# K^T V in two row tiles, a finer-grained first group and dummy matmuls, in linear attention followed by an ELU MLP

## The chip, the cores and the metric

The kernel runs on one core of a Trainium2 chip. The metric is the device time of one execution in microseconds (us). The span of a profile is about 2 us shorter than the time measured for the same run, so spans are compared with spans and times with times. Engines: PE is TensorE (matmuls), PEld its weight loads, DVE is VectorE, ACT is ScalarE, POOL is GpSimd, SP issues DMAs. PSUM is the memory that the matmuls write to, in banks. The chain of waits is a view of the profile: the work that ended last, followed back from each step to what released it. The timeline merges neighbouring instructions of one kind into a line; the trace keeps the start of each.

## The reference

```python
# q, k, v: (8 batches, 8 heads, 576 rows, 64); w_in: (512, 2048); w_out: (2048, 512)
kv  = einsum('bhsd,bhse->bhde', k, v)               # K^T V, 64x64 per head
out = einsum('bhsd,bhde->bhse', q, kv)
out = out / sqrt(mean(out*out, -1) + 1e-6) * g_norm # RMS norm per head
x   = out.transpose(0, 2, 1, 3).reshape(4608, 512)
h   = x @ w_in
g   = where(h > 0, h, exp(min(h, 0)) - 1)           # ELU
y   = g @ w_out
```

The kernel computes ELU as max(min(exp(h), 1) - 1, h). Matmul operands are bfloat16, sums float32.

## The kernel before

Work goes in nine groups of 512 rows: groups 0 to 7 are the first 512 rows of each batch, group 8 collects the last 64 rows of all eight. For each group the attention part makes x, transposed; then eight "h tiles" (two blocks of 128 of the 2,048 inner columns each) are computed, passed through ELU into gT, and multiplied by W_out ("o matmuls").

K and V of a batch are 576 = 4 x 128 + 64 rows: four full column blocks and a tail of 64 rows, loaded apart and multiplied last. The attention parts share one PSUM tile of two banks (`at`, one buffer), so they follow each other.

```python
def kv():                                  # K^T V of one group
    kv_ps = at_tile(FP32, 0)[:, 0:512].rearrange("p (r e) -> p r e", r=NPAIR)
    for p in range(NPAIR):                 # 4 pairs of heads
        for c in range(J + 1):             # 4 blocks of 128 rows, then the tail
            rows = P if c < J else TAIL    # 128, or 64
            nc.tensor.matmul(kv_ps[:, p, :],
                lhsT=k_sb[0:rows, c, 2*p:2*p+2, :], rhs=v_sb[0:rows, c, 2*p:2*p+2, :],
                start=(c == 0), stop=(c == J))
    ...                                    # diagonal blocks copied to bd_kv

def se(h):                                 # two row blocks of 128: q (K^T V), norm
    se_ps = at_tile(FP32, 0)...            # matmuls
    nc.scalar.activation(sq, se_ps, AF.Square)
    nc.vector.reduce_sum(out=ss, in_=sq...)
    ...                                    # ACT: Ln, Exp -> 1/rms
    nc.vector.tensor_tensor(out=xs..., in0=se_ps..., in1=ss.to_broadcast(...), op=ALU.mult)

def mm1(T, i):                             # h tile i of group T; ps_m1 has 2 buffers
    h_ps = ps_m1.tile([P, 2, G], FP32, name="h_ps", tag="mm1")
    ...                                    # 8 matmuls 128x128 by 128x512
    nc.scalar.activation(e, h_ps, AF.Exp)
    def rest():
        nc.vector.tensor_scalar(out=e, in0=e, ..., op0=ALU.min, op1=ALU.subtract)
        nc.vector.tensor_tensor(out=gT..., in0=e, in1=h_ps, op=ALU.max)

# schedule
at = attention(0)
for n in (1, 0, 2, 4, 6): at[n]()          # q, kv, se0, se1, x of group 0, one after the other
for i in range(8): mm1(0, i)()             # group 0's h loop: nothing else to run
...                                        # six halves of group 0's o with group 1's attention
for T in range(1, NT):                     # later: h of T, o of T-1, attention of T+1
    for i in range(8):
        rest = mm1(T, i); mm2(T - 1, i); rest()
        if i in at: at[i]()                # {0: kv, 1: q, 2: se0, 4: se1, 6: x}
```

Of the kernel before, what the change touches and what calls it, by code (L numbers as in the profile page):

```python
# [16 lines left out]
def kernel(  # L17
# [11 lines left out]

    nc = tc.nc  # L30
# [8 lines left out]
    TAIL = S - G  # L39
# [29 lines left out]
    nc.vector.memset(bd_kv, 0.0)  # L69
# [5 lines left out]
    def stage_tile():  # L75
        return stage.tile([P, 2048], FP32, name="st", tag="st")

    raw = {}

    def fetch_main(name, src, b):  # L80
        st = stage_tile()
        nc.sync.dma_start(
            out=st.rearrange("p (h x) -> p h x", h=H),
            in_=src[b, :, 0:G, :].rearrange("h (p j) d -> p h (j d)", j=J),
        )
        raw[name, b] = st

    def fetch_tail(name, src, b):
        st = stage.tile([TAIL, H, D], FP32, name="stt", tag="stt", bufs=4)
        nc.sync.dma_start(out=st, in_=src[b, :, G:S, :].rearrange("h p d -> p h d"))  # L90
        raw[name + "t", b] = st

    def fetch(b):
        fetch_main("q", q, b)
        fetch_main("k", k, b)
        fetch_tail("k", k, b)
        fetch_main("v", v, b)
        fetch_tail("v", v, b)

    def fetch_q_tails():  # L100
        st = stage_tile()
        sv = st.rearrange("p (i h d) -> p i h d", i=J, h=H)
        for b in range(B):
            nc.sync.dma_start(
                out=sv[(b % 2) * 64 : (b % 2) * 64 + 64, b // 2, :, :],
                in_=q[b, :, G:S, :].rearrange("h p d -> p h d"),
            )
        raw["q", B] = st

    def fetch_w_in(s):  # L110
        st = stage_tile()
        nc.sync.dma_start(
            out=st.rearrange("p (c f) -> p c f", c=KC),
            in_=moe_w_in.rearrange("(c p) f -> p c f", p=P)[:, :, s * 512 : s * 512 + 512],
        )
        raw["wi", s] = st

    def fetch_w_out(s):
        st = stage_tile()
        nc.sync.dma_start(  # L120
            out=st.rearrange("p (c f) -> p c f", c=KC),
            in_=moe_w_out.rearrange("(c p) f -> p c f", p=P)[:, 4 * s : 4 * s + 4, :],
        )
        raw["wo", s] = st

    bf = {}
# [7 lines left out]
    def cast(name, b, engs):  # L134

        t = qkvp.tile([P, J + 1, H, D], BF16, name=f"{name}_bf", tag=name)
        bf[name, b] = t
        st = raw.pop((name, b))
        if b < B:
            sv = st.rearrange("p (h j d) -> p j h d", h=H, j=J)  # L140
        else:
            sv = st.rearrange("p (j h d) -> p j h d", h=H, j=J)
        for j in range(J):
            copy_on(engs[j % len(engs)], t[:, j, :, :], sv[:, j, :, :])
        if name != "q":
            stt = raw.pop((name + "t", b))
            copy_on(engs[-1], t[0:TAIL, J, :, :], stt)

# [12 lines left out]

    def attention(T):
        st = {}

        def at_tile(dtype, n):
            full = ps_at.tile([P, 1024], FP32, name="at", tag="at")
            return full if dtype == FP32 else full.bitcast(BF16)

        def kv():
            if T == B:  # L170
                return
            k_sb, v_sb = bf.pop(("k", T)), bf.pop(("v", T))
            kv_ps = at_tile(FP32, 0)[:, 0:512].rearrange("p (r e) -> p r e", r=NPAIR)
            for p in range(NPAIR):
                for c in range(J + 1):
                    rows = P if c < J else TAIL
                    nc.tensor.matmul(  # L177
                        kv_ps[:, p, :],
                        lhsT=k_sb[0:rows, c, 2 * p : 2 * p + 2, :],
                        rhs=v_sb[0:rows, c, 2 * p : 2 * p + 2, :],  # L180
                        start=(c == 0),
                        stop=(c == J),
                    )
            nc.scalar.copy(bd_kv[0:64, T, :, 0:64], kv_ps[0:64, :, 0:64])
            nc.scalar.copy(bd_kv[64:128, T, :, 64:128], kv_ps[64:128, :, 64:128])

        def q_t():
            q_sb = bf.pop(("q", T))
            qt_ps = at_tile(BF16, 0).rearrange("p (r t) -> p r t", r=NPAIR)
            for p in range(NPAIR):  # L190
                for j in range(J):
                    nc.tensor.transpose(  # L192
                        qt_ps[:, p, j * P : j * P + P],
                        q_sb[:, j, 2 * p : 2 * p + 2, :],
                        ident,
                    )
# [5 lines left out]
        def se(h):  # L202
            def run():
                qT = st["qT"]
                se_ps = at_tile(FP32, 0).rearrange("p (c f) -> p c f", c=2)
                for c in range(2):
                    j = 2 * h + c
                    for p in range(NPAIR):
                        if T < B:
                            nc.tensor.matmul(  # L210
                                se_ps[:, c, p * P : p * P + P],
                                lhsT=qT[:, p, j * P : j * P + P],
                                rhs=bd_kv[:, T, p, :],
                                start=True,
                                stop=True,
                            )
                        else:
                            for l in range(2):
                                nc.tensor.matmul(
                                    se_ps[l * 64 : l * 64 + 64, c, p * P : p * P + P],  # L220
                                    lhsT=qT[:, p, j * P + l * 64 : j * P + l * 64 + 64],
                                    rhs=bd_kv[:, 2 * j + l, p, :],
                                    start=True,
                                    stop=True,
                                )
                sq = attp.tile([P, 2, DM], BF16, name="sq", tag="sq")
                nc.scalar.activation(sq, se_ps, AF.Square)  # L227
                ss = attp.tile([P, 2 * H], FP32, name="ss", tag="ss")
                nc.vector.reduce_sum(  # L229
                    out=ss, in_=sq.rearrange("p c (h e) -> p (c h) e", h=H), axis=AX.X  # L230
                )
                nc.scalar.activation(ss, ss, AF.Ln, bias=eps_col, scale=1.0 / D)  # L232
                nc.scalar.activation(ss, ss, AF.Exp, scale=-0.5)  # L233
                if h == 0:
                    st["xs"] = attp.tile([P, J, DM], BF16, name="xs", tag="xs")
                nc.vector.tensor_tensor(  # L236
                    out=st["xs"][:, 2 * h : 2 * h + 2, :].rearrange(
                        "p c (h e) -> p (c h) e", h=H
                    ),
                    in0=se_ps.rearrange("p c (h e) -> p (c h) e", h=H),  # L240
                    in1=ss.to_broadcast([P, 2 * H, D]),
                    op=ALU.mult,
                )
# [3 lines left out]
        def x_t():  # L247
            xs = st["xs"]
            xt_ps = at_tile(BF16, 0).rearrange("p (r t) -> p r t", r=NPAIR)
# [14 lines left out]
        return {0: kv, 1: q_t, 2: se(0), 4: se(1), 6: x_t}  # L264
# [4 lines left out]
    def mm1(T, i):  # L269
# [4 lines left out]
        for a in range(2):  # L274
            f = 2 * i + a
            for c in range(KC):
                nc.tensor.matmul(  # L277
                    h_ps[:, a, :],
                    lhsT=w_in_sb[:, c, f * P : f * P + P],
                    rhs=x[:, c, :],  # L280
                    start=(c == 0),
                    stop=(c == KC - 1),
                )
        e = mlpt.tile([P, 2, G], BF16, name="elu_e", tag="elu_e")
        nc.scalar.activation(e, h_ps, AF.Exp)  # L285

        def rest():
# [4 lines left out]
                out=gT[T][:, 2 * i : 2 * i + 2, :], in0=e, in1=h_ps, op=ALU.max  # L292
# [6 lines left out]
    def mm2(T, i):  # L299

        j, half = i // 2, i % 2
        if half == 0:
            o_ps[T] = ps_m2.tile([P, DM], FP32, name="o_ps", tag="mm2")
        for f in range(8 * half, 8 * half + 8):
            nc.tensor.matmul(  # L305
                o_ps[T],
# [5 lines left out]
        if half == 1:  # L312
            if j % 2 == 0:
                o_sb[T] = outp.tile([P, 2, DM], FP32, name="o_sb", tag="o")
            nc.scalar.copy(o_sb[T][:, j % 2, :], o_ps[T])  # L315
            if j % 2 == 1:
                store(T, j // 2)

# [18 lines left out]
    fetch(0)  # L337
    for s in range(4):
        fetch_w_in(s)
    cast("q", 0, [Q])  # L340
    cast("k", 0, [V])
    cast("v", 0, [V, A])
    for s in range(4):
        cast_w_in(s, Q)
    for s in range(4):
        fetch_w_out(s)
    fetch(1)
    at = attention(0)
    for n in (1, 0, 2, 4, 6):
        at[n]()  # L350
# [3 lines left out]
    def cast_all(b):  # L354
        cast("q", b, [Q])
        if b < B:
            cast("k", b, [Q])
            cast("v", b, [Q])

    cast_all(1)  # L360
    for i in range(8):
        mm1(0, i)()
    fetch(2)
    at = attention(1)
    for i, n in ((0, None), (1, 1), (2, 0), (3, 2)):
        mm2(0, i)
        if n is not None:
# [57 lines left out]
```

## Time and profile before

Median of three runs: 350.9 us (350.68 to 351.55). The profiled run took 352.89 us; its span is 351.1 us.

| stage | from, us | what sets the time |
|---|---|---|
| no h matmul yet | 0 to 36.8 | loads, then group 0's attention, one operation after the other |
| groups 0 and 1, not yet dense | 36.8 to 111.25 | waits between PE, ACT and DVE; slow TensorE clock in places |
| from group 2's h on | 111.25 to the end | PE without a gap almost from the start |

These are lines of the page: the busy share of PE, and the TensorE clock that the throttle granted, in tenths, in 40 equal slices (8.8 us each).

```profile
PE   0242778939968999999999999999999999999993
PEclk9999999996989999999999999999999999999998
```

PE is full from the fourteenth slice on (114 us). The clock row shows slow stretches in slices 10 (from 79 us) and 12 (from 97 us). It shows full speed at the start, where the matmuls' own durations say otherwise. Lines of the timeline, PE: start in us, duration, engine, line, operation, operands, count, and in brackets how long the engine had been idle and what ended that.

```profile
36.80 5.99 PE L277 MATMUL h_ps<-xT,w_in_sb 128*128 128x512 bf16 x16 [0.84 <-DVE xT L259]
43.60 1.89 PE L277 MATMUL h_ps<-xT,w_in_sb 128*128 128x512 bf16 x8 [0.81 <-DVE gT L291]
46.09 1.89 PE L277 MATMUL h_ps<-xT,w_in_sb 128*128 128x512 bf16 x8 [0.60 <-DVE gT L291]
...
77.62 1.05 PE L252 MATMUL at<-ident,xs 128*128 128x128 bf16 x16 [2.49 <-DVE xs L236]
79.52 3.87 PE L277 MATMUL h_ps<-xT,w_in_sb 128*128 128x512 bf16 x8 [0.84 <-DVE xT L259]
83.18 3.15 PE L305 MATMUL o_ps<-w_out_sb,gT 128*128 128x512 bf16 x8
```

Sixteen matmuls take 5.99 us, then eight take 1.89: at first the clock is about half. The same happens after the waits before 79.5 us. In between, each h tile waits for the DVE operation (L291) that empties one of the two PSUM buffers.

Two lines of the chain of waits in the dense part (start, duration, what):

```profile
147.84 1.85 PE at L177 x20
149.69 1.83 PE h_ps L277 x8
```

K^T V takes 1.85 us for 20 matmuls, 92 ns each, though 16 transposes of the same size take 0.89 us, 56 ns each.

### The profile page before, as it was taken

Reading aid. Unit: us, or ns where it says so; the run is one execution under the profiler, and the core shown is the slowest. Engines: PE = TensorE matmul, PEld = TensorE weight load, DVE = VectorE, ACT = ScalarE, POOL = GpSimd, SP = SyncE. Lnnn points to the kernel's source line nnn. Section 1 sums busy time; section 2 is a strip of 40 time slices with the busy share of each in tenths; the row PEclk is TensorE's granted clock in tenths of the full one; section 3 lists DMA queues with packets and bytes.
Section 4 is the critical chain, followed back from the end, with each engine's and each line's share of the span. In section 5 each row is a group of like instructions: output and inputs, shape, how many; then the busy total and the mean of one; then the engine's idle time right before and its main releaser. Section 6 shows DMA issues by size and latency. Waiting matters only on the chain.

```text
span 351.1 us, 4399 instructions
## 1 busy us (share of the span) xinstructions
PE 303.7 (86%) x1760; PEld 151.2 (43%) x1760; DVE 180.8 (52%) x207; ACT 145.9 (42%) x200; POOL 82.3 (23%) x144
## 2 busy tenths in 40 slices
PE   0242778939968999999999999999999999999993
PEld 0132333523524545554545455455545444544441
DVE  2214277152386567537636864675377467454500
ACT  1042333422545364445435643654454454434311
POOL 1158867326045000035006202600200000000000
PEclk9999999996989999999999999999999999999998
DMA  6999999094391000292078109513410101101022
GB/s 214 284 386 387 337 284 230 33 297 121 113 297 41 2 34 26 98 332 82 0 231 219 60 15 310 138 50 96 85 60 2 61 0 62 60 2 60 14 87 81
DMA packets 44916, 46.42 MB, mean 132 GB/s; under 512 B 13664, under 2 KB 38240, under 8 KB 44896
## 3 DMA queue, kind: packets, MB, share of 16 engines
q1 hardware_dynamic: 44736, 46.14, 43.8%
q8 instruction: 14, 0.23, 0.3%
q14 instruction: 6, 0.05, 0.0%
q10 hardware_dynamic: 160, 0.00, 0.0%
HBM read 36.70 MB, written 9.44 MB: 131 GB/s over the span
## 4 chain that ended last, share of the span: by engine, by line
PE 78%; DVE 8%; ACT 7%; DMA 4%; issue 1%; SPq 1%; DVEq 0%
PE h_ps L277 33%; PE o_ps L305 33%; PE at L177 5%; DMA st<-in_v_dram 4%; DVE gT L291 3%; PE at L252 2%; ACT elu_e L285 2%; PE at L210 2%; PE at L192 2%; DVE xs L236 2%; DVE ss L229 2%; DVE elu_e L288 1%; ACT sq L227 1%; ACT xT L262 1%; ACT qT L200 1%
## 5 line engine op out<-in xcount | busy, mean ns | idle before, releaser
L277 PE MATMUL h_ps<-xT,w_in_sb 128*128 128x512 bf16 x576 | 141.7, 390 | 8.8 <-DVE gT L291 5.7
L305 PE MATMUL o_ps<-w_out_sb,gT 128*128 128x512 bf16 x576 | 136.0, 382 | 0.1
L285 ACT ACTIVATE elu_e<-h_ps 128x1024 bf16<-128x1024 f32 x72 | 73.4, 1021 | 57.2 <-PE h_ps L277 57.2
L291 DVE TENSOR_TENSOR gT<-elu_e,h_ps 128x1024 bf16<-128x1024 bf16 x72 | 87.9, 1221 | 7.5
L277 PEld LDWEIGHTS <-w_in_sb 128*128 128x128 bf16 x576 | 55.8, 100 | 75.1 <-issue 15.1
L305 PEld LDWEIGHTS <-gT 128*128 128x128 bf16 x576 | 56.4, 98 | 68.7 <-issue 2.2
L288 DVE TENSOR_SCALAR elu_e<-elu_e 128x1024 bf16<-128x1024 bf16 x72 | 34.6, 480 | 93.3 <-ACT elu_e L285 93.1
L132 POOL CAST q_bf<-st 128x512 bf16<-128x512 f32 x36 | 21.5, 633 | 138.6 <-DMA st<-in_q_dram 118.9
L229 DVE TENSOR_REDUCE ss<-sq 128x16 f32<-128x1024 bf16 x18 | 21.9, 1219 | 21.8 <-ACT sq L227 21.8
L315 ACT COPY o_sb<-o_ps 128x512 f32<-128x512 f32 x36 | 21.0, 584 | 26.2 <-PE o_ps L305 26.2
L236 DVE TENSOR_TENSOR xs<-at,ss 128x1024 bf16<-128x1024 f32 x18 | 22.0, 1225 | 11.3 <-ACT ss L233 11.3
L227 ACT ACTIVATE sq<-at 128x1024 bf16<-128x1024 f32 x18 | 18.5, 1026 | 18.2 <-PE at L210 15.6
L177 PE MATMUL at<-v_bf,k_bf 128*128 128x128 bf16 (+1 forms) x160 | 17.2, 232 | 8.2 <-ACT qT L200 8.2
L262 ACT ACTIVATE xT<-at,g_col 128x1024 bf16<-128x1024 bf16 x9 | 10.0, 1115 | 24.1 <-DVE xT L259 24.1
L192 PE MATMUL at<-ident,q_bf 128*128 128x128 bf16 x144 | 10.9, 229 | 9.2 <-POOL q_bf L132 9.2
L132 POOL CAST v_bf<-st 128x512 bf16<-128x512 f32 x28 | 16.9, 641 | 8.4 <-DMA st<-in_v_dram 8.4
L132 POOL CAST k_bf<-st 128x512 bf16<-128x512 f32 x28 | 16.5, 629 | 9.0 <-DMA st<-in_k_dram 9.0
L210 PE MATMUL at<-bd_kv,qT 128*128 128x128 bf16 x128 | 10.5, 230 | 8.9 <-DVE xs L236 7.8
L177 PEld LDWEIGHTS <-k_bf 128*128 128x128 bf16 (+1 forms) x160 | 11.3, 100 | 15.7 <-issue 7.3
L232 ACT ACTIVATE ss<-ss,eps_col 128x16 f32<-128x16 f32 x18 | 5.6, 309 | 26.1 <-DVE ss L229 26.1
L252 PE MATMUL at<-ident,xs 128*128 128x128 bf16 x144 | 10.3, 229 | 6.7 <-DVE xs L236 6.7
L210 PEld LDWEIGHTS <-qT 128*128 128x128 bf16 x128 | 9.1, 103 | 12.9 <-issue 9.7
(28 smaller groups left out, 88.8 us busy)
## 6 DMA issues: line engine op xcount, KB each, us to landing
st<-in_q_dram SPq DMA_DIRECT2D x8, 1024.0 KB, 6.8
st<-in_k_dram SPq DMA_DIRECT2D x8, 1024.0 KB, 10.4
st<-in_v_dram SPq DMA_DIRECT2D x8, 1024.0 KB, 11.1
out_dram<-o_sb SPq DMA_DIRECT2D x16, 512.0 KB, 3.1
st<-in_moe_w_in_dram SPq DMA_DIRECT2D x4, 1024.0 KB, 11.7
st<-in_moe_w_out_dram SPq DMA_DIRECT2D x4, 1024.0 KB, 14.0
stt<-in_k_dram SPq DMA_DIRECT2D x8, 128.0 KB, 10.1
stt<-in_v_dram SPq DMA_DIRECT2D x8, 128.0 KB, 9.8
```

The source lines that it names most:

```text
L132: eng.tensor_copy(out=out_, in_=in_)
L177: nc.tensor.matmul(kv_ps[:, p, :], lhsT=k_sb[0:rows, c, 2 * p : 2 * p + 2, :], rhs=v_sb[0:rows, c, 2 * p : 2 * p + 2, :], start=(c == 0), ...
L210: nc.tensor.matmul(se_ps[:, c, p * P : p * P + P], lhsT=qT[:, p, j * P : j * P + P], rhs=bd_kv[:, T, p, :], start=True, stop=True,)
L227: nc.scalar.activation(sq, se_ps, AF.Square)
L229: nc.vector.reduce_sum(out=ss, in_=sq.rearrange("p c (h e) -> p (c h) e", h=H), axis=AX.X)
L236: nc.vector.tensor_tensor(out=st["xs"][:, 2 * h : 2 * h + 2, :].rearrange("p c (h e) -> p (c h) e", h=H), in0=se_ps.rearrange("p c (h e) - ...
L277: nc.tensor.matmul(h_ps[:, a, :], lhsT=w_in_sb[:, c, f * P : f * P + P], rhs=x[:, c, :], start=(c == 0), stop=(c == KC - 1),)
L285: nc.scalar.activation(e, h_ps, AF.Exp)
L288: nc.vector.tensor_scalar(out=e, in0=e, scalar1=1.0, scalar2=1.0, op0=ALU.min, op1=ALU.subtract)
L291: nc.vector.tensor_tensor(out=gT[T][:, 2 * i : 2 * i + 2, :], in0=e, in1=h_ps, op=ALU.max)
L305: nc.tensor.matmul(o_ps[T], lhsT=gT[T][:, f, j * P : j * P + P], rhs=w_out_sb[:, f, :], start=(f == 0), stop=(f == FC - 1),)
L315: nc.scalar.copy(o_sb[T][:, j % 2, :], o_ps[T])
```

## The change

The intent: (1) K and V as 9 rows by head parity on all 128 partitions, so that no tail is left, loads come in 2,304-byte runs, and K^T V becomes pairs of 64-row matmuls in the upper and lower half of the array, writing two PSUM banks; (2) group 0's attention by 128-row subtiles over more PSUM banks, to overlap its steps; (3) dummy matmuls that keep the TensorE clock up; (4) a new schedule for groups 0 and 1, with quarters of the o matmuls as filling, and every second h tile of group 0 finished by way of a Relu on ACT.

```diff
-            for p in range(NPAIR):
-                for c in range(J + 1):
-                    rows = P if c < J else TAIL
-                    nc.tensor.matmul(kv_ps[:, p, :], lhsT=k_sb[0:rows, c, ...], ...)
+    def kv_mm(T, kv_ps, u):                     # called for u = 0, 1
+        for j in range(RK):                     # 9 rows
+            for s in range(2):                  # head parity = half of the partitions
+                rows = slice(s * 64, s * 64 + 64)
+                nc.tensor.matmul(kv_ps[s][:, u * P : u * P + P],
+                    lhsT=bf["k", T][rows, j, 2 * u : 2 * u + 2, :],
+                    rhs=bf["v", T][rows, j, 2 * u : 2 * u + 2, :],
+                    start=(j == 0), stop=(j == RK - 1))
 ... (group 0, new)
+    def idle(n):
+        for _ in range(n):
+            nc.tensor.matmul(idle_ps[:, 0, :], lhsT=ident, rhs=zeros, start=True, stop=True)
+    idle(16)
 ... (q casts and transposes, idle(2) twice; K and V casts on DVE and ACT; kv_mm,
      idle(6) after the first; bd_kv copies; idle(3); row outputs of 4 subtiles; idle(10))
+    norm_a(0); norm_a(1); norm_b(0); norm_a(2); turn(0); norm_b(1); norm_a(3)
+    turn(1); norm_b(2); turn(2); norm_b(3); turn(3)   # idle(2) after turn(1) and turn(3)
 ... (h tiles)
+        if relu:                                # odd tiles of group 0
+            nc.scalar.activation(h, h_ps, AF.Relu)   # then DVE adds instead of max
 ... (schedule)
+    at["kv"]()
+    for s, n in enumerate(("se0", "se1", None, "x")):  # group 1's attention
+        for j in range(2): mm2(0, j, 4 * s, 4 * s + 4) # quarters of o
+        if n: at[n]()
+    steps = {1: "q", 2: "kv", 3: "se0", 5: "se1", 7: "x"}   # group 2, in group 1's h loop
 ... (from group 2 on as before)
```

## The prediction

> **What bounds the kernel now.** The span is 351.1 us and has three parts.
> - 0 to 36.8 us: no MLP matmul at all. The chain of waits runs from the V load (its last piece lands at 17.1 us) through casts, K^T V, and two rounds of square (1.03), sum (1.23), scale (1.24), to the first h matmul at 36.8.
> - 36.8 to 113.8 us: TensorE is busy but gated. Group 0's h tiles come every 2.44 us (timeline: exponentials at 40.71 to 57.77) though eight matmuls take 1.73; group 1's h waits until 79.5, group 2's until 111.25. Some runs on a slow clock: the first sixteen h matmuls take 374 ns each against 216 later, and again after the wait at 77 us (granted clock 0.86).
> - 113.8 to 345.6 us: TensorE 100% busy (busy time by stretch), 32.2 us per group: 16 x 1.73 for the MLP, 1.85 for K^T V, 0.89 each for q and x transposes and for the row outputs.
>
> **What the change does.**
> 1. First group's load: K and V in 2,304-byte runs instead of 1,024 plus 256-byte tails, in front of the weights, in halves. Before, 0 to 10 us moved 2.2 MB; later stretches reach 0.37 to 0.39 MB/us. Estimate: q by 6.2 us, V by 12.6 instead of 17.1.
> 2. Group 0 by subtile: half-size square, sum and scale overlap over four row groups in three tile pools. Laid out in engine order with half the measured durations, the first h matmul starts at 24.7 (estimate), 12 us earlier. The dummy matmuls keep the clock up: another 2 to 2.5 us.
> 3. Group 0's h loop: Relu on ACT for every second tile shortens DVE, but the other tile's loop, 1.73 + 1.02 + 0.43 + 1.22 + handoffs, still sets 4.7 to 4.8 us a pair (was 4.9). Done at about 43 instead of 57.7.
> 4. Group 1's attention with o matmuls in quarters between: chain about 14 us, was 22. Group 1's h at 57 (was 79.5). This needs w_out cast by 44 to 47 us; loads (11 MB by 45 us) just allow it.
> 5. Group 1's loop: 31.7 us before with 3 us of slow clock; it now carries 7 quarters of o, so about 28.5. Group 2's h at about 85.5: 26 us earlier.
> 6. K^T V in two row tiles. Twenty matmuls take 1.85 us, but twenty at the transposes' 56 ns would be 1.1: the four 64-row ones cost the rest. The Trainium skill, "TensorEngine Tiling (Array Packing)", Key Properties, says that changing the tiling mode drains the engine and that tiles run in parallel. So eighteen pairs at 56 ns plus one change in and out: 1.2 us, 0.65 saved in each of the five dense groups, 3.2 in all. If the tiles don't overlap: 2.2, a loss.
>
> Sum: 26 + 3.2 = 29 us off. **Predicted 322 us, range 313 to 331.** Faster by over 2%: 0.97; within: 0.02; slower: 0.01.
>
> **What would show it.** First h matmul at 23 to 27 us, 216 ns from the start; first group-1 h at 55 to 60; dense from 83 to 89 on, 31.5 us per group; K^T V 1.0 to 1.4 us per group; no matmul at 374 ns after the first dummies.
>
> **What would make it wrong.** Row tiles that don't overlap (+5 us); w_out or group 2's loads too late for groups 0 and 1 (+3 to 8); DVE slowed while GpSimd casts; or a group-1 loop that interleaved quarters bring near its 24.5 us of TensorE work (-4).

## The result, and the profile after

The changed kernel takes 330.15 us (median of 4 runs, 329.64 to 331.94), against 351.23 us of before in the same rounds. A ratio is always the mean time of one kernel's fast runs over that of the other's of the same rounds, so not quite the ratio of the medians quoted. Here it is 0.9403, with a 95% interval of 0.9356 to 0.945. The predicted 322 is 8 us too low; the time is just inside the range of 313 to 331. That it is inside is partly luck: the same code, run again as a control (below), took 331.43. Of the signs that the prediction named, h at 23 to 27 us, 31.5 us per dense group and K^T V came true in this profile; full speed from the first h matmul, group 1's h by 60 us and a dense part from 89 us at the latest did not.

Starts of the stages, in us, from the timelines:

| | before | predicted | after |
|---|---|---|---|
| first h matmul of group 0 | 36.80 | 24.7 | 26.56 |
| end of group 0's h matmuls | 57.6 | 43 | 47.2 |
| first h matmul of group 1 | 79.52 | 57 | 61.74 |
| first h matmul of group 2 | 111.25 | 85.5 | 90.92 |
| from there to the end of the span | 239.85 | 236.6 | 237.4 |

So 20.3 us of the 22.8 us by which the span shrank are gained before group 2, and 2.5 after it. The page's rows after (slices of 8.2 us):

```profile
PE   8648796799789999999999999999999999999993
PEclk9996999999979999999999999999999999999999
```

The PE row is high from the first slice, but there it is dummies. The clock row has two dips: in slice 4, where group 0's h starts, and in slice 12, where group 2's starts. PE on the timeline:

```profile
21.16 0.59 PE L404 MATMUL idle_ps<-zeros,ident 128*128 128x512 bf16 x2
22.71 0.40 PE L467 MATMUL xt_ps<-ident,xs 128*128 128x128 bf16 x4 [0.95 <-DVE xs L238]
25.04 0.61 PE L467 MATMUL xt_ps<-ident,xs 128*128 128x128 bf16 x4 [1.94 <-DVE xs L238]
25.45 1.06 PE L404 MATMUL idle_ps<-zeros,ident 128*128 128x512 bf16 x2
26.56 5.29 PE L313 MATMUL h_ps<-xT,w_in_sb 128*128 128x256 bf16 x24
...
47.18 1.18 PE L182 MATMUL at<-v_bf,k_bf 64*128 64x128 bf16 x36
...
87.82 1.03 PE L347 MATMUL o_ps<-w_out_sb,gT 128*128 128x512 bf16 x4
90.92 0.59 PE L313 MATMUL h_ps<-xT,w_in_sb 128*128 128x512 bf16 x2 [2.07 <-DVE xT L294]
92.06 2.72 PE L313 MATMUL h_ps<-xT,w_in_sb 128*128 128x512 bf16 x6 [0.55 <-ACT xT L297]
```

Two dummies take 0.59 us at 21.16 and 1.06 us at 25.45: the clock was lost between. Group 0's h then starts slowly, as it did before the change, in spite of 43 dummies. (The code has 43 and the control's trace below shows all of them; this trace has records of 41.) Busy time by stretch says the same (stretch, length, then busy us and instruction counts of PE, PEld, DVE, ACT and POOL, granted clock, DMA share, GB/s):

```profile
26.50:30.10 3.60, 3.54 (x18) 2.44 (x17) 0.00 (x0) 0.00 (x0) 2.86 (x6) 0.52 1.06 390
```

The last three lines of the timeline above show a new wait: group 2's x is now the last thing in group 1's loop, PE waits 2.07 + 0.55 us for it (0.66 + 0.56 before the change), and the six h matmuls after it run on the slow clock (2.72 us; 1.46 in a warm case).

Group 0's h loop, ACT on the timeline (L321 exponential, L325 Relu):

```profile
30.16 1.02 ACT L321 ACTIVATE elu_e<-h_ps 128x1024 bf16<-128x1024 f32 x1 [5.90 <-PE h_ps L313]
31.89 1.02 ACT L321 ACTIVATE elu_e<-h_ps 128x1024 bf16<-128x1024 f32 x1 [0.70 <-PE h_ps L313]
32.81 1.02 ACT L325 ACTIVATE elu_h<-h_ps 128x1024 bf16<-128x1024 f32 x1
35.38 1.02 ACT L321 ACTIVATE elu_e<-h_ps 128x1024 bf16<-128x1024 f32 x1 [1.55 <-PE h_ps L313]
37.10 1.02 ACT L321 ACTIVATE elu_e<-h_ps 128x1024 bf16<-128x1024 f32 x1 [0.70 <-PE h_ps L313]
38.02 1.02 ACT L325 ACTIVATE elu_h<-h_ps 128x1024 bf16<-128x1024 f32 x1
40.46 1.02 ACT L321 ACTIVATE elu_e<-h_ps 128x1024 bf16<-128x1024 f32 x1 [1.42 <-PE h_ps L313]
```

The first tiles of the pairs come at 30.16, 35.38 and 40.46: 5.1 to 5.2 us a pair, slower than the 4.9 of before. From its first h matmul to its end the loop takes 20.6 us (47.2 - 26.56), before 20.8: all the change in this loop bought next to nothing.

K^T V in the dense part, from the chain of waits:

```profile
128.12 1.11 PE at L182 x36
129.24 0.32 PE h_ps L313
129.56 0.05 issue
129.61 1.46 PE h_ps L313 x6
```

1.11 us, 0.74 less than before; the h tile behind it still takes 1.83 us.

### The profile page after: what moved, and what is told of

Its sections match the earlier page's. It is cut to its first block, busy times and chain, and to the rows that moved or that the text cites. A ratio compares the mean times of both kernels' runs of the same rounds, so it can differ in the third digit from the quotient of the medians.

```text
span 328.3 us, 4746 instructions
## 1 busy us (share of the span) xinstructions
PE 299.2 (91%) x1903; PEld 151.0 (46%) x1939; DVE 180.3 (55%) x216; ACT 152.1 (46%) x216; POOL 78.5 (24%) x140
## 4 chain that ended last, share of the span: by engine, by line
PE 76%; DVE 7%; DMA 7%; ACT 4%; POOL 2%; issue 2%; SPq 1%; DVEq 0%
PE o_ps L347 34%; PE h_ps L313 33%; DMA st<-in_k_dram 4%; DMA st<-in_v_dram 3%; PE at L182 2%; DVE gT L331 2%; PE at L287 2%; PE at L204 2%; DVE ss L228 2%; DVE xs L238 2%; PE at L192 2%; POOL v_bf L137 1%; DVE elu_e L328 1%; ACT elu_e L321 1%; POOL k_bf L137 1%
## 5 line engine op out<-in xcount | busy, mean ns | idle before, releaser
L313 PE MATMUL h_ps<-xT,w_in_sb 128*128 128x512 bf16 (+1 forms) x565 | 136.3, 383 | 9.6 <-DVE xT L294 2.9
L321 ACT ACTIVATE elu_e<-h_ps 128x1024 bf16<-128x1024 f32 x72 | 73.4, 1021 | 57.0 <-PE h_ps L313 55.5
L238 DVE TENSOR_TENSOR xs<-at,ss 128x1024 bf16<-128x1024 f32 (+1 forms) x18 | 21.0, 1166 | 10.8 <-ACT ss L235 10.8
L228 DVE TENSOR_REDUCE ss<-sq 128x16 f32<-128x1024 bf16 (+1 forms) x20 | 22.2, 1112 | 8.2 <-ACT sq L223 8.0
L223 ACT ACTIVATE sq<-at 128x1024 bf16<-128x1024 f32 (+1 forms) x18 | 17.5, 977 | 17.0 <-PE at L204 14.4
L137 POOL CAST k_bf<-st 128x512 bf16<-128x512 f32 (+1 forms) x35 | 19.8, 608 | 6.6 <-DMA st<-in_k_dram 6.6
L137 POOL CAST v_bf<-st 128x512 bf16<-128x512 f32 (+1 forms) x35 | 19.2, 592 | 0.5
L404 PE MATMUL idle_ps<-zeros,ident 128*128 128x512 bf16 x41 | 13.1, 460 | 1.6 <-POOL ident masks.py:199 1.4
L267 ACT COPY qT<-at 128x1024 bf16<-128x1024 bf16 x8 | 8.1, 1012 | 11.4 <-DVE qT L266 11.4
L137 POOL CAST w_in_sb<-st 128x512 bf16<-128x512 f32 x16 | 9.1, 613 | 17.1 <-DMA st<-in_moe_w_in_dram 17.1
L182 PEld LDWEIGHTS <-k_bf 64*128 64x128 bf16 x288 | 8.2, 94 | 7.1 <-issue 3.9
```

Of the source, the lines that this page charges most:

```text
L137: eng.tensor_copy(out=out_, in_=in_)
L182: nc.tensor.matmul(kv_ps[s][:, u * P : u * P + P], lhsT=bf["k", T][rows, j, 2 * u : 2 * u + 2, :], rhs=bf["v", T][rows, j, 2 * u : 2 * u + ...
L228: nc.vector.reduce_sum(out=ss, in_=sq.rearrange("p c (h e) -> p (c h) e", h=H), axis=AX.X)
L238: nc.vector.tensor_tensor(out=xs.rearrange("p c (h e) -> p (c h) e", h=H), in0=se_ps.rearrange("p c (h e) -> p (c h) e", h=H), in1=ss.to_b ...
L313: nc.tensor.matmul(h_ps[:, a, cs], lhsT=w_in_sb[:, c, f * P : f * P + P], rhs=x[:, c, cs], start=(c == 0), stop=(c == KC - 1),)
```

## The experiments

Twelve kernels ran, each in 5 rounds with the kernel before on the same chip; all were correct. The changed kernel ran again as a control, at a ratio of 0.9432, against 0.9403 at first: the same code differs by 0.3%, 1 us. Smaller differences of time are not read here; the profiles resolve more.

### Do the row tiles overlap?

```diff
-        for j in range(RK):
-            for s in range(2):
+        for s in range(2):
+            for j in range(RK):
```

> The changed kernel, but in K^T V all nine matmuls of the one row tile come first, then all nine of the other, so that neighbours never belong to different tiles. Theory A (the two row tiles overlap): K^T V of a later group goes from 1.11 us to 36 x 56 ns = 2.0 us or more, about 0.9 us in each of the five dense groups, in all +4 to +6 us on the time. Theory B (the gain came only from the four changes of tile size that the old order had; the tiles don't overlap): still 1.11 us, time unchanged within 1 us.

Measured: 333.48 us, ratio 0.9482 (0.9454 to 0.9511). From the chain of waits of this kernel:

```profile
130.67 1.50 PE at L182 x36
132.17 1.83 PE h_ps L313 x8
```

K^T V takes 1.50 us: neither 1.1 nor 2.0. The starts of the single matmuls in the traces say why. In the changed kernel the two matmuls of a pair start 3 to 4 ns apart, and the pairs follow every 56 ns: the two tiles do run in parallel. In this run most starts lie 56 ns apart, but after the first six of each nine come starts in between, 8 to 19 ns behind a neighbour. That fits nine matmuls of the next tile beginning while the former tile still has three to go, each tile at its own 56 ns. Three such overlaps of three leave 27 steps of 56 ns, 1.51 us. So theory A holds; its 2.0 us failed because the edit did not keep the tiles fully apart.

By the ratios the time is 1.8 us (against the control) to 2.8 us (against the first run) longer, not 4 to 6; about 2 us of it (5 x 0.39) come from K^T V. In this profile h also started 1.7 us later than in the changed kernel's first profile: V's second half was cast 0.7 us later, dummies on the slow clock held back the second half of K^T V by another 0.7, and K^T V itself took 0.3 longer.

### Was it the parallel tiles, or the changes of tile size?

The kernel before, tails filled up with zeros:

```diff
+            nc.gpsimd.memset(t[TAIL:P, J, :, :], 0.0)
             copy_on(engs[-1], t[0:TAIL, J, :, :], stt)
...
-                    rows = P if c < J else TAIL
+                    rows = P
```

> The kernel before, with the 64-row tails of K and V filled up with 64 rows of zeros (written by GpSimd), so that all twenty matmuls of K^T V have 128 rows; no row tiles anywhere. Theory B (the cost was in going to and from 64-row matmuls): K^T V falls from 1.85 to 20 x 56 ns = 1.1 us, as low as the changed kernel's 1.11, and the time by 3.5 to 5 us (0.990 to 0.986 of before). Theory A alone (only running tiles in parallel helps): still 1.85 us, time unchanged.

Measured: 344.53 us against 351.88, ratio 0.9807 (0.978 to 0.9833): faster, though whether by 2% is unclear. From its chain of waits:

```profile
142.63 1.12 PE at L178 x20
143.75 1.73 PE h_ps L278 x8
```

Two changed lines, for 64 rows of zeros, in the kernel before make K^T V as short as the two row tiles do (1.12 against 1.11), and the h tile behind it is back at 1.73, which the row tiles don't reach. Together that is 0.83 us a group, against 0.74 for the row tiles. Shown: the old cost was that of going to 64 rows and back, four times a group, about 0.21 us each time (0.83 / 4). The single starts in the trace of the kernel before agree: a full matmul follows a full one after 56 ns, a 64-row one follows a full one after 152, and a full one follows a 64-row one after 158 to 160, so each way costs about 0.1 us; a 64-row matmul is not slow in itself, since in a row they too come every 56 ns. With row tiles one change in and one out remain in each group; with zeros all twenty starts of a K^T V lie 56 ns apart. The parallel tiles only make up for using half the array.

The time fell by 7.35 us, more than the 3.5 to 5 expected. In this profile group 2's h starts 4.4 us earlier (106.89 against 111.25), of which 1.4 are already there at group 1's h, and the rest is group 1's loop: 28.8 against 31.7 us. The slow-clock stretch fell on the eight o matmuls at 71.8 (2.97 us) and was over when group 1's h began at 78.1 (1.46 us for six h matmuls). So a slow stretch moved from the critical h matmuls to others; that a shift of some tenths of a us caused it is likely and not shown. From group 2's h on the rest is 236.0 us against 239.85, 3.8 us less, near the 4.2 us of five groups.

### How much is the load, how much the subtiles?

Group 0's attention in whole tiles through the one `at` tile, with the new loads, casts, row tiles and schedule, and without dummies:

```diff
-    (the subtile block of group 0, dummies)
+    at = attention(0)
+    at["q"]()
+    (K and V casts as in the changed kernel)
+    for n in ("kv", "se0", "se1", "x"):
+        at[n]()
```

> The changed kernel with its new loads, row tiles and schedule, but group 0's attention done in whole tiles through the one shared PSUM tile as in the kernel before, and no dummy matmuls. Mine: the load layout and casts give most of the 10.2 us by which h starts earlier; h starts at 29 to 31 us (26.6 in the changed kernel, 36.8 before), time +2.5 to +5 us against the changed kernel. Rival (the subtile pipeline gives most of it): h starts at 33 us or later, time +7 us or more.

Measured: 333.58 us, ratio 0.9485 (0.946 to 0.951). From its timeline:

```profile
14.59 1.14 PE L182 MATMUL at<-v_bf,k_bf 64*128 64x128 bf16 x18 [1.86 <-DVE v_bf L137]
27.00 1.86 PE L287 MATMUL at<-ident,xs 128*128 128x128 bf16 x16 [4.21 <-DVE xs L238]
29.71 0.59 PE L313 MATMUL h_ps<-xT,w_in_sb 128*128 128x256 bf16 x2 [0.84 <-DVE xT L294]
```

The first h matmul comes at 29.71, as expected. The kernel before with padded tails has the same whole-tile attention and as short a K^T V, and starts h at 36.02: so loads, casts and their order are worth 6.3 us. The subtile pipeline is worth 2.7: with it, and also without dummies, h starts at 27.02 (the next run). By the ratios the time is 1.9 to 2.9 us longer than the changed kernel's. Half-size operations cost more than half: the scaling by g on ACT takes 0.69 us for 512 columns and 1.11 for 1,024, the row scaling on DVE 0.69 and 1.22.

### What are the dummies worth?

```diff
-        for _ in range(n):
+        for _ in range(0):
```

> The changed kernel without any of the 41 dummy matmuls. Mine: they don't reach their aim, since h starts on the slow clock with them too (225 ns for 256 columns; granted clock 0.52 from 26.5 to 30.1); without them the few matmuls of group 0's attention run at half speed, which costs 0.3 to 1.5 us. Rival, as the prediction had it: they are worth 2 to 2.5 us. Second rival: they are worth nothing or cost time, 0 to -0.5 us.

Measured: 330.53 us, ratio 0.9394 (0.9369 to 0.9419), the same as with them. Its timeline:

```profile
27.02 5.49 PE L313 MATMUL h_ps<-xT,w_in_sb 128*128 128x256 bf16 x24
47.09 1.18 PE L182 MATMUL at<-v_bf,k_bf 64*128 64x128 bf16 x36
```

h starts at 27.02 (26.56), its first exponential at 30.68 (30.16), and 16 us later, at 47.09 (47.18), the loops end together. The second rival is right: the 43 dummies are worth nothing within noise. Dummies do move the clock, but they stand in TensorE's queue in front of real work. The control's profile, the same code as the changed kernel, shows it:

```profile
11.50 1.26 PE L182 MATMUL kv_ps<-v_bf,k_bf 64*128 64x128 bf16 x18 [2.87 <-DVE v_bf L137]
12.69 2.52 PE L404 MATMUL idle_ps<-zeros,ident 128*128 128x512 bf16 x6
15.14 0.68 PE L182 MATMUL kv_ps<-v_bf,k_bf 64*128 64x128 bf16 x18
```

Six dummies at half clock take 2.52 us and hold back the second half of K^T V. It starts at 15.14, though the casts that it needs end at 14.52; in the other profile of this code it started with the end of its casts, at 14.02. So 0.6 us of the delay are the dummies', and 0.5 are V, which arrived later. In the control h starts at 27.68, not 26.56. Where the clock falls differs from run to run; why is left open.

The control:

> The changed kernel again, unedited, as a control for the two others of this call: ratio 0.937 to 0.943 to the kernel before, h of group 0 first at 26.5 to 28 us.

Measured: 331.43 us, ratio 0.9432 (0.9399 to 0.9466), as told above; h first at 27.68.

More dummies in the gaps where the clock was lost:

```diff
-            idle(2)                    # after turn(1) and turn(3)
+        idle((8, 6, 8, 2)[j])          # after every turn(j)
```

> The changed kernel with more dummies after each of the four last transposes of group 0 (8, 6, 8, 2 instead of 0, 2, 0, 2), in the gaps from 18.5 to 25 us in which the clock was lost. Theory C (the slow clock at the start of group 0's h is worth what it shows): h tile 0 takes 1.8 instead of 3.6 us, the loop ends 1.5 us earlier, time -1 to -2 us. Rival (the loop behind it absorbs it, as it seems to with no dummies at all): within 0.5 us.

Measured: 328.54 us, ratio 0.9366 (0.934 to 0.9392). Its timeline has all 24 matmuls of the first two h tiles on the full clock (5.29 us in the changed kernel):

```profile
27.54 3.63 PE L313 MATMUL h_ps<-xT,w_in_sb 128*128 128x256 bf16 x24
```

h tile 0 takes 1.94 us (27.54 to the exponential at 29.48) and not 3.6; group 1's h comes at 61.02. That is 0.7 us earlier than in the changed kernel's first profile and 2.5 us earlier than in the control's (63.48). Theory C holds, with 1.3 to 2.3 us by the ratios (against the first run and against the control); the lower value is hardly more than the 1 us by which the same code differs.

The same late dummies without the early ones:

> The changed kernel with the dummies only where the run with more of them had added some: 8, 6, 8 and 2 after the four last transposes of group 0, none before. In several traces the early dummies ran on the slow clock and stood in front of K^T V and of the row outputs in TensorE's queue (h first at 27.5 to 28.2 us in those, 26.6 to 27.0 otherwise). Mine: h first at 26.8 to 27.3, tile 0 done 1.9 us later instead of 3.6, time -1.5 to -2.5 us against the control. Rival (the early ones are needed to have the clock at 24 us): tile 0 takes 3 us or more, time within 0.7 us of the control.

Measured: 332.06 us, ratio 0.9444 (0.9412 to 0.9477), not better than the control. A miss of mine. Its timeline:

```profile
20.27 3.62 PE L404 MATMUL idle_ps<-zeros,ident 128*128 128x512 bf16 x8
23.68 0.63 PE L461 MATMUL xt_ps<-ident,xs 128*128 128x128 bf16 x4
24.11 2.10 PE L404 MATMUL idle_ps<-zeros,ident 128*128 128x512 bf16 x6
```

The eight dummies, now on the slow clock, take 3.62 us, and the next transposes wait for them; h starts at 29.25. It is then warm, but 2 us late.

### What paces group 0's h loop?

Without the Relu:

```diff
-        mm1(0, i, cols, relu=(i % 2 == 1))()
+        mm1(0, i, cols, relu=False)()
```

> The changed kernel, but in group 0's h loop no Relu on ScalarE: every tile is finished by VectorE from PSUM, as before. Theory P (the loop is paced by the two PSUM buffers, and an even tile's own path, matmuls, exponential, minimum, maximum, is what holds one): pace stays 5.0 to 5.2 us a pair, time 0 to +1 us. Theory D (VectorE's load paces the loop): a pair takes 0.5 us more on VectorE, pace 5.5 us or more, time +1.5 to +2.5 us.

Measured: 331.52 us, ratio 0.9442 (0.941 to 0.9474), the control's within noise. From the first exponential (31.16) to K^T V of group 1 (48.25) the loop takes 17.1 us; with the Relu 17.0 (30.16 to 47.18). (The first two pairs take 4.8 us each, less than the 5.0 to 5.2 expected, and the rest of the loop more.) So DVE's load does not pace the loop. With a third place for h, in two single PSUM banks that the o matmuls don't need yet:

```diff
+        if third:                      # tiles 2 and 5 of group 0
+            hs = [ps_m2.tile([P, G], FP32, name="h3_ps", tag="mm2") for _ in range(2)]
+        else: ...                      # as before; exponential and rest by halves if third
```

> The changed kernel with a third place for h in group 0's loop: tiles 2 and 5 use the two single-bank PSUM tiles that the o matmuls don't need yet. Theory P: the pace falls from 5.1 us a pair towards VectorE's and TensorE's load of 3.4 to 3.7, the loop ends at 42 to 44 us instead of 47.2, time -3 to -4.5 us. Theory D: pace and time within 1 us of the changed kernel.

Measured: 328.46 us, ratio 0.9361 (0.933 to 0.9392). Its timeline:

```profile
27.79 12.51 PE L317 MATMUL h_ps<-xT,w_in_sb 128*128 128x256 bf16 x56
44.97 1.18 PE L182 MATMUL at<-v_bf,k_bf 64*128 64x128 bf16 x36 [0.33 <-ACT qT L267]
```

PE now runs through the 56 h matmuls of the first six tiles without a gap that the timeline shows. The same stretch takes 13.6 us (31.40 to 44.97). Theory P holds: the PSUM buffers paced the loop. (The edit also does tiles 2 and 5 by halves; what that alone is worth was not tested.) The expected end, 42 to 44, missed by 1 us because h started at 27.79 in this profile. Of the 3.4 us, the time shows 1.5 (against 0.9403) to 2.5 (against the control). The profiles lose nothing of it later on: against the control's, where h started at nearly the same time (27.68), the loop ends 3.4 us earlier, group 2's h starts 3.9 us earlier (88.95 against 92.86), behind the same two waits of 2.07 and 0.55 us, and the span is 3.7 us shorter. The ratios are means over runs in which the slow stretches fall differently.

### The late x of group 2

```diff
-    steps = {1: "q", 2: "kv", 3: "se0", 5: "se1", 7: "x"}
+    steps = {0: "q", 1: "kv", 2: "se0", 4: "se1", 6: "x"}
```

> The changed kernel with group 2's attention one h tile earlier in group 1's loop (after tiles 0, 1, 2, 4, 6 instead of 1, 2, 3, 5, 7). In the changed kernel TensorE waits 2.07 + 0.55 us for group 2's x and then runs six h matmuls in 2.72 us on the slow clock. Theory X (x comes last, with nothing left behind it to run): wait and slow clock go, time -2 to -3.5 us. Rival (the loop as a whole is bound by VectorE and ScalarE, the wait only moves): within 1 us.

Measured: 327.65 us, ratio 0.9327 (0.9298 to 0.9356), 2.7 to 3.7 us less. Its timeline:

```profile
89.29 0.59 PE L313 MATMUL h_ps<-xT,w_in_sb 128*128 128x512 bf16 x2
90.17 1.46 PE L313 MATMUL h_ps<-xT,w_in_sb 128*128 128x512 bf16 x6 [0.29 <-ACT xT L297]
```

Group 1's loop takes 26.9 us (62.37 to 89.29) against 29.2, the wait is down to 0.29 us, the six matmuls run warm, and the rest from 89.29 on takes 235.8 us against 237.4. Theory X holds.

### Together

Third place for h, earlier attention of group 2, late dummies only:

> Late dummies only, a third place for h in group 0's loop, and group 2's attention one tile earlier, together. If the three faults are separate in time, the gains add: loop ends at 42 to 43.5 us (47.2), group 1's h at 56 to 58 (61.7), group 2's h at 83 to 86 (90.9), time -6 to -8 us against the control, 322 to 325 us. Rival (a later step, the W_out or group 2 loads or their casts on GpSimd, takes part of it back): -3 to -5 us.

Measured: 323.63 us, ratio 0.9218 (0.9183 to 0.9253), 7.5 us below the control (0.0214 x 352). The loop ends at 43.7, group 1's h starts at 58.53, group 2's at 85.48. The first two just miss their windows, since h starts only at 28.21 (late dummies again); the third and the gain are in the expected range.

Then with only as many dummies as fit into the gaps when the clock is slow:

```diff
-        idle((8, 6, 8, 2)[j])
+        idle((4, 3, 4, 2)[j])
```

> As the run with all three edits, but 4, 3, 4 and 2 dummies after the four last transposes of group 0 instead of 8, 6, 8 and 2: no more than fit into each gap (2.1, 1.4, 2.1 us) at the slow clock's 0.43 us. Mine: they delay nothing, h first at 26.8 to 27.4 us instead of 28.2, and keep TensorE busy enough that h tile 0 takes 2.5 us or less; ratio to the kernel before 0.917 to 0.921. Rival (with gaps between them the clock stays low): tile 0 takes 3 us or more and the ratio is 0.921 or more.

Measured: 322.42 us, ratio 0.9177 (0.9147 to 0.9207). Its timeline:

```profile
24.53 1.53 PE L412 MATMUL idle_ps<-zeros,ident 128*128 128x512 bf16 x4
26.67 0.40 PE L469 MATMUL xt_ps<-ident,xs 128*128 128x128 bf16 x4 [0.61 <-DVE xs L238]
27.56 10.54 PE L317 MATMUL h_ps<-xT,w_in_sb 128*128 128x256 bf16 x55
29.50 1.02 ACT L327 ACTIVATE elu_e<-h_ps 128x1024 bf16<-128x1024 f32 x1 [3.61 <-PE h_ps L317]
```

h starts at 27.56, a little later than expected, and tile 0 takes 1.94 us: warm. 13 dummies do what 43 could not. Whether they gain over the run with 24 is within noise. This version beats the kernel before by 8.2% and the changed kernel by 2.4% to 2.7% (0.9177 over 0.9403 or 0.9432).

## Why the prediction was right or wrong

Direction, and most of the mechanism, were right; the size, 29 us, was 8 us too large. Nearly 2 us of that are no error of a step: the predicted 29 us were counted off the median time of 350.9, while the stages were read from a profile whose run took 352.89. The other 6.2 us are in these terms of the sum (spans):

1. First group's load and subtiles: h at 24.7 predicted, 26.56 measured, 1.9 late. V's last part landed at 13.4 us, not 12.6 (its cast began at 13.7 to 14.2 in the other profiles with these loads), and half-size operations cost more than half (0.69 for 1.11 and 1.22 us). Loads 6.3 and subtiles 2.7 us: the load was the larger part.
2. **"The dummy matmuls keep the clock up: another 2 to 2.5 us." This step failed.** They don't cover the stretch from 21.75 to 25.04, h tile 0 takes 3.6 us instead of about 1.8, and without any dummies the time is the same.
3. Group 0's h loop: that the even tile's own path sets the pace, and that the Relu gains little, was right and is shown by the run without Relu and the one with a third place. The pace, 5.1 and not 4.75 us, was mis-sized: the minimum on DVE takes 0.73 to 0.85 us for even tiles where GpSimd casts at the same time, 0.43 otherwise. The prediction had named this among what would make it wrong, but its sum takes 0.43. Steps 1 to 3 give 1.9 + 1.8 + 3 x 0.35 = 4.7 us; measured 47.2 against 43.
4. Group 1's attention: 14.6 us, predicted 14. The W_out casts were in time: the last ended at 47.83, the first o matmul came at 48.30.
5. Group 1's loop: 29.2, predicted 28.5. It ends in a wait that nobody had counted, for x as its last product.
6. K^T V: 1.11 us, predicted 1.2, so 0.74 and not 0.65 a group; 5 x 0.74 = 3.7. Only 2.5 came through, since group 2 started on the slow clock (six matmuls in 2.72 us instead of 1.46). That the 64-row matmuls cost by changing the tile size was right, and so was that the tiles overlap; but 64 rows of zeros would have done as much without row tiles.

A remark on step 3: the Trainium skill, "SBUF — State Buffer", section "Who interferes with whom", says that DVE operations such as `tensor_scalar` in their fast modes contend with GpSimd for a shared pair of ports, and that a DVE operation with at most one SBUF input outside those modes does not. The traces agree: in the changed kernel the minimum varies from 0.42 to 0.87 us, over 0.43 only with GpSimd casts running; the maximum, which reads one operand from PSUM, is always 1.22. That the ports are the cause no run here isolates.

## What to carry to other kernels

Before splitting an odd-sized contraction into parallel tiles, try to pad it: here the cost was in switching sizes, and part of it sat in the instruction behind. Dummy matmuls are work in TensorE's queue, and the real ones behind them waited; on the slow clock they took twice as long (3.62 us for eight, 1.89 on the full clock). So put in no more than fit into the gap at the slow rate, and put them into the last gaps before the work that is to be warm. When a stage is filled and still slow, look for what arrives last and for how many buffers the loop turns over, before taking load off an engine.

## What the Trainium skill lacked or had wrong

- "TensorEngine Tiling (Array Packing)", Key Properties, says that changing the tiling mode drains TensorE, but gives no number. Here a switch from 128-row to 64-row matmuls and back cost about 0.21 us (K^T V 1.85 to 1.12 us and the h tile behind it 1.83 to 1.73, for four such switches, once the tails were padded), 0.1 us each way.
- The same page, Theoretical Speedup, gives up to 2x for a contraction of 64 or less, and doesn't name padding as the alternative. Here 36 half matmuls in two row tiles took 1.11 us, and 20 full ones with zeros 1.12. Alternating the tiles mattered (1.11 against 1.50 us).
- "TensorE: Matmul & The Clock Gate", section "Why this matters for your kernels", asks for no idle gap above about 3 us. Here the clock was lost with no gap above 1.94 us: PE was busy 1.62 of the 6.5 us from 18.5 to 25.0. With PE busy 6.63 of 7.7 us in short pieces (19.8 to 27.5, the last run) it had risen by 26.7. So 3 us is no safe bound when short gaps follow each other. These two stretches suggest that the busy share counts, not the longest gap alone; no run isolates it.
- The same page, Part 4, says that the full clock doesn't engage for transposes and gives about 275 ns each in a kernel. Here 16 transposes of 128x128 between other matmuls take 0.89 us, one every 56 ns, and on the timeline 1.05 us (77.62, kernel before) against 1.86 on the slow clock (27.00, whole tiles): the full clock did serve them. The profile gives 229 ns for one, nearer to the page's figure; which mode they run in, and whether transposes alone raise the clock, no run here shows.
- The same page, "Back-to-back issue gap", gives 131 ns for each matmul of 512 columns in a sustained stream with weight loads. Here eight take 1.73 us, one every 216 ns, as its formula for an isolated gap has it.
- No page warns that warm-up matmuls delay the real ones behind them: here eight took 3.62 us on the slow clock, and h started 2.2 us later (29.25 against 27.02 with none).
